# Where VectorE's small work stands between a kernel's matmuls: seven moves in one instruction order

## The chip, the cores and the metric

One NeuronCore of a Trainium2 chip runs the whole kernel. The metric is the device time of one execution in microseconds (us). The kernel before takes 943.9 us (median of three runs, 943.89 to 946.26).

A core has engines that run at the same time, each through its own list of instructions: TensorE multiplies matrices (PE in the profile, PEld for its weight loads), VectorE (DVE) does elementwise work, reductions and 32x32 block transposes, ScalarE (ACT) exponentials and copies, GpSimd (POOL) here mostly indirect DMAs, and SyncE (SP) issues DMAs. They wait for one another by semaphores. SBUF is the working memory; TensorE writes its results to PSUM, from where VectorE or ScalarE reads them.

## The reference

Attention in which a query sees only the keys of its own cluster, followed by a two-layer network with a PReLU. There are 4 batches, 8 heads, 768 tokens, head size 64 and 16 clusters for each head.

```python
q_assign = argmax(normalised(q) @ normalised(centroids).T)      # and k_assign, for each head
mask = q_assign[:, :, :, None] == k_assign[:, :, None, :]
scores = where(mask, q @ k.T / 8, -1e9)
attn = softmax(scores)                                          # over the keys
x = heads_side_by_side(attn @ v)                                # 3072 x 512
h = x @ w_in                                                    # 512 x 2048
out = (maximum(h, 0) + alpha * minimum(h, 0)) @ w_out           # 2048 x 512
```

## The kernel before, in words

**Pairs and steps.** Two heads of one batch make a pair; pair n is heads 2(n%4) and 2(n%4)+1 of batch n//4, so there are 16. Pairs 0 to 9 are worked on as they lie, once for each half of the queries. Pairs 10 to 15 are first sorted by cluster ("whole" or "near" pairs), so that each chunk of 128 keys meets only a window of the queries around it. The order of the work is written out by hand as 78 steps u, three to a pair and half (or to a whole pair). Steps 0 to 23 are batch 0; 24 to 47 batch 1; 48 to 53 pairs 10 and 11; 54 to 65 pairs 8 and 9; 66 to 77 pairs 12 to 15. TOGETHER is 24.

**Slots.** A step is divided into slots. In each slot `tick()` first runs what was put off with `later(k, piece)` (k ticks ahead), then come VectorE's pieces of attention, then `feed(pieces)`, which issues pieces of the network of earlier rows, then `prepare(u, slot)`, which issues what `prep_at` holds for that place. In the first step of a pair from step 24 on there are three ticks around the scores and only two such slots, and there `prepare` comes right after the tick, for places 2 and 3 (FIRST is 2): what is put at place 2 has no network piece of its step ahead of it, and what is put at place 3 comes behind those that the first slot feeds. How many pieces a slot feeds is worked out so that a block's pieces are spread evenly over its slots (L1557 to L1559). A hidden piece is one of 16 column blocks of w_in (8 matmul instructions, L1063) with a copy by ScalarE (L1069) and a slope by VectorE (L1055); a final piece is 8 instructions of L1081.

**Attention of a pair.** The scores (L781) go to PSUM, ScalarE takes exponentials (L799, L802), VectorE masks (L822) and adds up (L832, L860, L864), turns the sums (L870) and reduces them (L878). At the head of the next pair's first step TensorE folds the sums (L891), VectorE inverts them (L904) and spreads them (L911), TensorE weighs the values (L936, or L969 for whole pairs) and VectorE multiplies both (L1039, L975).

**Clusters.** `prep_blocks` (L364) transposes the queries and keys of a pair, `prep_sims` (L381) multiplies them by the centroids into the PSUM bank "mps", and one tick later VectorE takes the argmax (L402 to L408). The pool of mps has one buffer; `misc()` hands it out, and its next user waits until its last reader is done. Whole pairs are ordered ahead of time: step ORDERS[n-10] loads them, the next transposes them (`order_features`, L565), the one after multiplies (`order_sims`, L573) and takes the argmax piece by piece in the following slots; eight and nine ticks on come a transpose and a running count (L587), then `order_begins` (L599), `order_ranks` (L607 to L609), `order_rows` (L616 to L620) and `order_clusters` (L637 to L643). GpSimd scatters their rows by these numbers (L673), a few in each slot, paced by tiny copies of ScalarE and GpSimd (L649, L650).

**Back to rows.** The result of a whole pair is turned on TensorE through mps (`to_rows`, L999, six ticks after the pair is normalised), copied by ScalarE one tick later (L1002), scattered back (L1008), fetched, and turned by VectorE (L1027).

**Checks.** The kernel's short cuts hold only if the inverses lie in a range and sorted clusters do not spread too far. `check_inverses` (L340, two reductions) keeps the smallest and largest of a batch, and the end combines all into a flag (L1582 to L1635) that decides whether a general version must run.

**The last batch.** Its network runs as a scheme with seven products instead of eight, after the attention. In `last_pieces`, `hidden(x)` for x = 0 to 7 has the products p1, p5, p2, p6, p3, p7 and, put off to the next x's p2, p4 (L1241). Their results are copied by ScalarE (L1173) or added by VectorE (L1176), then sloped (L1181), and p7 also issues sums for later products (L1220, L1229, L1126). After x = 7, `room_for_y` issues p4 at once. The final products follow (L1297).

## Time and profile before

| what | us |
|---|---|
| median of three runs | 943.9 |
| the profiled execution, its own time | 944.23 |
| its span, from the first to the last instruction | 942.5 |
| TensorE busy | 924.1 |
| VectorE busy | 663.5 |
| GpSimd busy | 351.2 |
| ScalarE busy | 265.9 |

The granted TensorE clock is 0.999 of full speed over the span. Busy times are averages over stages that differ. In the table by stage VectorE is busy for 22.47 of the 24 us from 448 to 472, 9.82 of the 10 from 472 to 482, 20.93 of the 24 from 508 to 532 and 55.76 of the 74 from 789 to 863; TensorE for 24.00, 7.91, 22.42 and 73.05 of them. Step 51 begins near 470 us, step 54 near 508, step 57 near 532, and the last batch's network at 789.

In the timeline and in groups of instructions a line names engine, source line, operation, what is written and read, and the number of instructions; in brackets stand the engine's idle time before it and what ended it. A matmul in fp32 is two instructions. The ends of matmuls are modelled, so their starts say more.

### The profile page before, as it was taken

Reading aid. Unit: us, or ns where it says so; the run is one execution under the profiler, and the core shown is the slowest. Engines: PE = TensorE matmul, PEld = TensorE weight load, DVE = VectorE, ACT = ScalarE, POOL = GpSimd, SP = SyncE. Lnnn points to the kernel's source line nnn. Section 1 sums busy time; section 2 is a strip of 40 time slices with the busy share of each in tenths; the row PEclk is TensorE's granted clock in tenths of the full one; section 3 lists DMA queues with packets and bytes.
Section 4 is the critical chain, followed back from the end, with each engine's and each line's share of the span. In section 5 each row is a group of like instructions: output and inputs, shape, how many; then the busy total and the mean of one; then the engine's idle time right before and its main releaser. Section 6 shows DMA issues by size and latency. Waiting matters only on the chain.

```text
span 942.5 us, 11891 instructions
## 1 busy us (share of the span) xinstructions
PE 924.1 (98%) x3995; PEld 496.5 (53%) x3995; DVE 663.5 (70%) x1247; ACT 265.9 (28%) x658; POOL 351.2 (37%) x529
## 2 busy tenths in 40 slices
PE   8999999999999999999999999999999999999997
PEld 5534444445455454454544545545455555556886
DVE  5797788799679589698995955456888535698100
ACT  5764444323123032331322322223133121221000
POOL 2333222200016576467534686364256670000000
PEclk9999999999999999999999999999999999999999
DMA  8333658039001645165920134333441112000000
GB/s 297 125 127 96 146 130 149 18 59 198 1 6 53 159 87 133 47 120 131 155 52 12 43 80 101 63 67 62 93 75 34 32 37 53 1 0 1 23 23 26
DMA packets 209668, 73.38 MB, mean 78 GB/s; under 512 B 194288, under 2 KB 198080, under 8 KB 209600
## 3 DMA queue, kind: packets, MB, share of 16 engines
q1 hardware_dynamic: 201840, 60.35, 29.2%
q0 software_dynamic: 6912, 11.81, 4.1%
q8 instruction: 33, 0.54, 0.2%
q10 hardware_dynamic: 848, 0.39, 0.2%
q14 instruction: 35, 0.29, 0.1%
HBM read 49.89 MB, written 22.28 MB: 77 GB/s over the span
## 4 chain that ended last, share of the span: by engine, by line
PE 87%; DVE 6%; SPq 2%; DMA 2%; issue 1%; POOL 1%; ACT 1%; ACTq 0%; DVEq 0%; POOLq 0%
PE fps L1081 26%; PE fps L1063 25%; PE vps L936 7%; PE sps L781 7%; PE sps L1297 4%; PE sps L1241 4%; PE fps L781 2%; PE vps L1297 2%; PE vps L1241 2%; PE fps L1297 1%; PE fps L1241 1%; PE sps L790 1%; PE vps L969 1%; PE mps L969 1%; PE mps L381 1%
## 5 line engine op out<-in xcount | busy, mean ns | idle before, releaser
L1063 PE MATMUL fps<-xT,w_in_sb 128*128 128x384 f32 x768 | 257.7, 490 | 0.0
L1081 PE MATMUL fps<-w_out_sb,gT 128*128 128x512 f32 x576 | 254.4, 595 | 1.1 <-DVE gT L1055 1.1
L1063 PEld LDWEIGHTS fps<-xT,w_in_sb 128*128 128x128 f32 x768 | 142.8, 190 | 102.6 <-issue 3.8
L1081 PEld LDWEIGHTS fps<-w_out_sb,gT 128*128 128x128 f32 x576 | 107.5, 190 | 133.4 <-issue 123.0
L673 POOL DMA_INDIRECT scratch<-stage,off x144 | 155.4, 1079 | 49.7 <-issue 25.1
L650 POOL COPY paced<-pace 1x1 f32<-1x1 f32 x196 | 55.5, 283 | 202.3 <-ACT pace L649 201.5
L1069 ACT COPY gT<-fps 128x384 f32<-128x384 f32 x96 | 46.0, 479 | 215.6 <-PE fps L1063 215.6
L1055 DVE SCALAR_TENSOR_TENSOR gT<-gT,alpha 128x384 f32<-128x384 f32 x96 | 61.3, 648 | 50.4 <-ACT gT L1069 50.3
L781 PE MATMUL sps<-qkT 64*128 64x384 f32 (+1 forms) x480 | 88.6, 487 | 0.0
L1008 POOL DMA_INDIRECT back<-rows,found x72 | 74.9, 1040 | 18.2 <-issue 16.1
L802 ACT ACTIVATE E<-sps 128x768 f32<-128x768 f32 (+1 forms) x78 | 57.9, 790 | 59.4 <-PE sps L790 38.8
L781 PEld LDWEIGHTS sps<-qkT 64*128 64x128 f32 x480 | 42.7, 186 | 40.5 <-issue 15.0
L822 DVE SCALAR_TENSOR_TENSOR more<-aq,key,more 128x384 f32<-128x384 bf16 (+2 forms) x120 | 63.0, 584 | 1.2 <-ACT more L799 1.1
L936 PE MATMUL vps<-E,vt 128*64 128x384 f32 x316 | 58.6, 495 | 1.4 <-DVE xT L1039 1.4
L904 DVE RECIPROCAL inverses<-mps 64x12 f32<-64x12 f32 (+1 forms) x44 | 10.9, 248 | 58.5 <-PE mps L891 58.1
L822 DVE SCALAR_TENSOR_TENSOR E<-aq,key,E 128x384 f32<-128x384 bf16 (+2 forms) x96 | 50.2, 577 | 1.9 <-ACT E L799 1.8
L271 POOL TENSOR_TENSOR w_in_sb<-w_in_sb,power 128x512 f32<-128x512 f32 x16 | 25.1, 1573 | 67.8 <-DVE w_in_sb L268 67.8
L832 DVE TENSOR_TENSOR acc<-acc,E 128x768 f32<-128x768 f32 x37 | 35.3, 953 | 14.7 <-ACT E L802 13.6
L271 POOL TENSOR_TENSOR w_out_sb<-w_out_sb,power 128x512 f32<-128x512 f32 x16 | 22.9, 1434 | 57.3 <-DVE w_out_sb L268 57.3
L802 ACT ACTIVATE more<-sps 128x768 f32<-128x768 f32 (+1 forms) x42 | 31.1, 775 | 33.1 <-PE sps L781 32.0
L1087 ACT COPY y<-fps 128x512 f32<-128x512 f32 x18 | 10.6, 586 | 99.1 <-PE fps L1081 99.1
L1089 DVE TENSOR_TENSOR y<-y,fps 128x512 f32<-128x512 f32 x24 | 16.4, 683 | 29.1 <-PE fps L1081 29.1
(283 smaller groups left out, 1167.2 us busy)
## 6 DMA issues: line engine op xcount, KB each, us to landing
raw<-in_moe_w_in_dram SPq DMA_DIRECT2D x16, 512.0 KB
raw<-in_moe_w_out_dram SPq DMA_DIRECT2D x16, 512.0 KB
out_dram<-y SPq DMA_DIRECT2D x21, 256.0 KB
qk<-in_q_dram SPq DMA_DIRECT2D x48, 96.0 KB
qk<-in_k_dram SPq DMA_DIRECT2D x48, 96.0 KB
qk<-scratch SPq DMA_DIRECT2D x48, 96.0 KB
w_in_kept<-w_in_sb SPq DMA_DIRECT2D x8, 512.0 KB
vt<-in_v_dram SPq DMA_DIRECT2D x10, 384.0 KB
```

The costliest lines, as they stand in the source:

```text
L650: nc.gpsimd.tensor_copy(out=sorts["paced"], in_=token)
L673: nc.gpsimd.indirect_dma_start(out=scratch[n][1][h * NX + xx], out_offset=bass.IndirectOffsetOnAxis(ap=ranks[n][:, xx, h:h + 1], axis=0), ...
L781: nc.tensor.matmul(out=bank(ps, h, m), lhsT=qkT[r:r + D, S + c * P:S + (c + 1) * P], rhs=qkT[r:r + D, tokens], start=True, stop=not early_ ...
L802: nc.scalar.activation(out=E[:, :, 0:m], in_=ps[:, :, 0:m], func=AF.Exp, scale=SCALE)
L822: nc.vector.scalar_tensor_tensor(out=e, in0=of, scalar=keys[n][:, NJ + c, h:h + 1], in1=e, op0=ALU.is_equal, op1=ALU.mult)
L936: nc.tensor.matmul(out=po[r:r + D, 0:HS], lhsT=vts[n][:, h, c, :], rhs=e[:, h, :], start=(c == 0), stop=(c == NJ - 1))
L1008: nc.gpsimd.indirect_dma_start(out=to[i], out_offset=bass.IndirectOffsetOnAxis(ap=place[:, h, j:j + 1], axis=0), in_=rows[j // HJ][:, j % ...
L1055: nc.vector.scalar_tensor_tensor(out=gs[f], in0=gs[f], scalar=alpha[:, f:f + 1], in1=gs[f], op0=ALU.mult, op1=ALU.max)
L1063: nc.tensor.matmul(out=ps[:, 0:HS], lhsT=w_in_sb[:, c, f * P:(f + 1) * P], rhs=xTs[b, half][:, c, :], start=(c == 0), stop=(c == NCH - 1))
L1081: nc.tensor.matmul(out=ps[:, 0:DM], lhsT=gs[f][:, i * P:(i + 1) * P], rhs=w_out_sb[:, f, :], start=on and f == f0, stop=off and f == f0 + ...
L1241: nc.tensor.matmul(out=bank[to], lhsT=w_in_form(m, x, cc), rhs=rhs[:, cc, :], start=start and cc == 0, stop=cc == KH - 1, skip_group_check ...
L1297: nc.tensor.matmul(out=bank[to], lhsT=g_form(m, x, t), rhs=w_out_form(n, x), start=start and x == 0, stop=x == NQ - 1, skip_group_check=no ...
```

## The change

Nothing is computed otherwise; instructions of VectorE, with what belongs to them, stand at other places.

- The range check of a batch is issued three ticks after the last inverse of that batch is asked for, at steps 24, 48 and 66. Before, it was issued when the first inverse of the next batch was asked for, just ahead of it, at steps 27, 51 and 69. The last batch's check stays at the end.
- The transposes of pair 6 (`prep_blocks` at step 23) go one slot later.
- The similarities of pairs 8 and 9 (`prep_sims` at steps 48 and 51) go from place 2 to place 3.
- The ordering of pair 15 begins at step 53 instead of 50: its eight loads, two transposes, similarities, argmax, count, ranks, rows and clusters all come three steps later.
- In the last batch's network the slopes of f1 are issued after p7's sum instead of p3's.
- The final check's small operations are spread between network pieces: eight pieces, not one, are fed before the `feed(8)` ahead of the flag.

```diff
-    kept_of = [0]
+    kept_of, inverted = [0], [0] * B
 
     def inverse(n, half):
 
-        if pairs[n][0] > kept_of[0]:
-            check_inverses()
+        b = pairs[n][0]
+        inverted[b] += 1
+        if inverted[b] == 2 * NCH and b < B - 1:
+            later(3, check_inverses)
         return inverses[:, (2 * n + half) % (2 * NCH), :]
...
             def p3():
                 plus(g_of(f1, 1), product("e", "S4", x_of(1, 1), False))
-                slopes(f1)
 
             def p7():
                 plus(g_of(f2, 1), product("a", "S3", x_of(1, 0), False))
+                slopes(f1)
                 late.append(p4)
...
-    ORDERS = [26, 29, 35, 38, 41, 50]
+    ORDERS = [26, 29, 35, 38, 41, 53]
...
                 for w in range(2):
-                    at(u - 7, FIRST + w, lambda n=n, w=w: prep_blocks(n, w))
+                    at(u - 7, FIRST + w + (u - 7 == TOGETHER - 1),
+                       lambda n=n, w=w: prep_blocks(n, w))
             at(u - (3 if n < NCH else 5 if u - 6 < TOGETHER else 6), FIRST,
-               lambda n=n: prep_sims(n))
+               lambda n=n: prep_sims(n)) if u - 6 < 2 * TOGETHER else at(
+                   u - 6, FIRST + 1, lambda n=n: prep_sims(n))
...
     sum_x(slice(0, 4))
+    feed(2)
     good = const.tile([P, 2], FP32, name="good")
     check_inverses()
+    feed(1)
     nc.vector.tensor_reduce(out=good[:, 0:1], in_=highest, axis=AX.X, op=ALU.max)
...
                             scalar2=good[:, 0:1], op0=ALU.is_ge, op1=ALU.mult)
+    feed(1)
     nc.vector.tensor_reduce(out=good[:, 0:1], in_=alpha, axis=AX.X, op=ALU.max)
...
-    feed(1)
+    feed(2)
     nc.vector.tensor_copy(out=spans.rearrange("p i n -> p (i n)"), in_=ps[0:m, 0:4 * NN])
...
+    feed(2)
     tiles = const.tile([m, 2, NN], I32, name="tiles")
```

## The prediction

> **What bounds the kernel now.** I read the page's first part, then TensorE's waits, then the timeline and the chain around the longest of them. From the page:

> ```profile
> PE 924.1 (98%) x3995; PEld 496.5 (53%) x3995; DVE 663.5 (70%) x1247; ACT 265.9 (28%) x658; POOL 351.2 (37%) x529
> ```

> TensorE sets the end. A piece of its work that waits for nobody cannot be shortened by another order, so the change can save no more than TensorE's waits for others. All of over 0.8 us (columns: waiter, released by, total us, times, longest):

> ```profile
> PE fps L354 <- ACT qkT L358: 1.6, 2, 1.5
> PE mps L599 <- DVE simT L587: 1.6, 1, 1.6
> PE vps L936 <- DVE xT L1039: 1.4, 1, 1.4
> PE vps L201 <- POOL ident masks.py:199: 1.4, 1, 1.4
> PE mps L381 <- DVE qk L975: 1.2, 1, 1.2
> PE fps L1081 <- DVE gT L1055: 1.1, 2, 0.9
> PE sps L1241 <- DVE gT L1176: 0.9, 1, 0.9
> PE mps L969 <- DVE inverses L904: 0.9, 1, 0.9
> ```

> Five of them (1.6, 1.2, 0.9, 0.9, 0.9, together 5.5 us) lie behind VectorE where the diff touches its order; the other three are in the first 70 us, where it changes nothing. The two around 475 us, in the timeline (start, length, engine, line, idle before and its releaser):

> ```profile
> 473.12 0.58 DVE L1055 SCALAR_TENSOR_TENSOR gT<-gT,alpha 128x384 f32<-128x384 f32 x1
> 473.62 0.25 DVE L340 TENSOR_REDUCE lowest<-inverses 128x1 f32<-128x96 int32 x1
> 473.78 0.24 DVE L340 TENSOR_REDUCE highest<-inverses 128x1 f32<-128x96 int32 x1
> 474.13 0.62 DVE L904 RECIPROCAL inverses<-mps 64x24 f32<-64x24 f32 x2
> 474.90 1.79 PE L969 MATMUL mps<-E,vt 128*64 128x384 f32 x16 [0.93 <-DVE inverses L904]
> 479.01 0.55 DVE L975 TENSOR_TENSOR qk<-mps,rd 128x384 f32<-128x384 f32 x1
> 479.61 0.85 PE L381 MATMUL mps<-qkT,cT 128*32 128x384 f32 x8 [1.16 <-DVE qk L975]
> ```

> The one PSUM bank "mps" ties both: the weighing of L969 and the similarities of L381 may not write it before VectorE has read it. The chain of work has the same picture at 194.59 and 861.68, VectorE just ahead of TensorE:

> ```profile
> 193.00 0.94 DVE qkT L364
> 193.94 0.51 DVE gT L1055
> 194.45 0.14 issue
> 194.59 1.96 PE fps L1081 x4
> ```

> [...] L904 starts only after both L340. [...] L381 starts 0.05 us after L975 ends. [...] the trace has 557 (L975) and 949 to 954 (L832). [...] I count starts: a 384-column instruction follows its predecessor by 0.322 us when nothing waits.

> **The change part by part**, in the profiled execution's time (944.23 us; span 942.5, 1.7 around it). Steps and slots are those told above.

> (a) Pair 6's two transposes (L364, 0.94 us each) go one slot later in step 23. The first no longer stands ahead of the slopes L1055. VectorE's reduction L878 ends at 192.59, L477 takes it to 193.08, the first slope ends at 193.6, TensorE resumes 0.15 later as now: 193.76 for 194.59, **0.83**. Behind this VectorE carries the same work; it waited 0.52 us for TensorE at 210.27 and 0.96 at 225.83, so the lead is kept.

> (b) The check of batch 1 (two L340) leaves the front of L904 at step 51: L1055 ends at 473.70, L904 could start at 473.66 for 474.13, **0.47**; 0.44 of the wait stays, because VectorE has no idle stretch over 0.1 us from 455 on. Its new place is step 48, after the first masks, where VectorE idled 0.36 us before L402 at 454.34; the two overlapping reductions need 0.36. Without that cover it would cost what it gains. The checks of batches 0 and 2 stood and will stand where VectorE is ahead of TensorE (it waited 0.96 us behind the first of them): nothing; with that cover gone, 0.36 each.

> (c) Pair 9's similarities go to the second slot of step 51. The first slot feeds one hidden piece there: after slot k of block 48 to 60 there remain 2 + ceil(26(47-k)/48) pieces, 22 at k=11, 21 at 12, 21 at 13. So 2.58 us of L1063 come ahead of L381; their PSUM banks are free, ScalarE's L799 being done at 478.22. L381 would have started at 478.51 (0.42 after the last score, as at an unstalled change of line): 479.61-478.51, **1.10**. Pair 8 at step 48 feeds nothing between its two places: nothing. Its argmax then follows the mask of chunk 4, the same sum on VectorE. Next to want mps after L381 is L999 two slots on, at 484.1 by then; VectorE's L402, freed of the transposes of (d), has read it by 482.5.

> (d) Pair 15's ordering goes from steps 50-55 to 53-58. The scan L587 (0.95) leaves step 54, so L599's wait there goes: it would have started at 516.1 for 517.74, **1.64**. It returns at step 57, where slot k=36 feeds a hidden piece (9 to 8 left) ahead of it. VectorE there: removed from 54-56 are scan 0.95, ranks 0.9, rows 1.3, clusters 1.45, together 4.6; added are two L565 of 0.96 and L402 to L410 at 0.58+0.55+0.59+0.36+0.55+0.54, together 5.1. Followed slot by slot, the scan would end near 541.9, L599 be reached near 542.3: no wait, by 0.4 us. But a new wait comes at step 55, slot 2: its rows (L999) are turned through mps, no piece is fed (13 left at k=27 and 28), and the moved similarities L573 want mps next. ScalarE's copy L1002 frees it 0.57 us after L999's end by 521.42+0.49 against 521.33, behind the copy L1069; L573 would start at 521.96 for 521.17, **-0.79**. Bounds: 0.45 if L1002 were not behind L1069, 0.95 with another entry ahead of it. All of TensorE's later work is queued behind L573; VectorE, full there, uses the time. The eight loads move on SyncE past the staging loads of step 51; their issue (0.5 to 0.7 each) then lies in steps 51-53 where nothing is staged, about 30 us before their use. The scatters don't move: pair 14's are 27 of the 51 after 543 us, and pair 15's begin near 600.

> (e) slopes(f1) goes from p3 behind p7's sum. Only for the last x is p4 right behind p7: L1176 could start at 860.84 (0.59 after p7's last matmul start, as at 859.55) for 861.08, and TensorE gains 0.23. The slopes, which now fill a hole, come after it, so the rest of VectorE's list runs 0.85 later: the last T1 (L1229, 871.95) ends at 872.8, when TensorE wants it (869.98+14*0.216=873.0, less 0.23). Between 0 and 0.23: **0.15**. For the other x the sums come earlier and VectorE's least margin (1.4 us, p3's sum at x=3) stays positive with 0.8 off.

> (f) The final check's 23 small operations (0.14 to 0.28 each, 4.5 us with their gaps from 789.62 to 794.12) go between the sums of six products of TensorE. It takes 1.29 us for each product and never waited from 790 to 859; at most nine of them, some 1.5 us, now stand ahead of one sum (p7's, at 797), whose reader p4 comes 3.9 us after the product's end. So nothing; without that cover, up to 0.3. The four matmuls L1596 (0.4 us) and L1632 only change place on TensorE.

> Sum: 0.83+0.47+1.10+1.64-0.79+0.15 = 3.40, so 940.83 for that execution. It was 0.33 over the median; from the median, 943.9-3.4 = **940.5**.

> **Rivals.**
> 1. More: L573's wait is short and all else holds: 4.2, 939.7. For it: L1002 takes only 0.49. Against it: L1069 is just ahead of it.
> 2. Given back: TensorE runs early into stretches where VectorE is full (22.5 of 24 us in 448-472, 20.9 of 24 in 508-532). If VectorE is 1 us later at step 57 than I count, L599 waits 0.6; if the check of batch 1 finds no hole, (b) is gone; with (e) at 0 the gain is 3.4-0.6-0.47-0.15, about 2.2: 941.7, no measurable change.
> 3. Slower: L1002 stuck behind ScalarE's pacing copies. ScalarE waited 5.1 us for GpSimd in three such copies at 551 to 555. If that happened just ahead of L1002 at step 55, L573 would wait 5.1 us more: 945.6. It decides when GpSimd is eight copies behind at 519 us; the timeline has it three behind, so it is unlikely.
> 4. A late load of pair 15 would hold VectorE's whole queue at L565; it would have to land 30 us late. Left out.

> **How the numbers follow.** A run tells about 0.3% from no change, 2.8 us: the line is 941.1. My case (940.0 to 941.3) 0.56, the first rival 0.15, the second 0.23, the third 0.06. The first is faster, nine tenths of mine too (a tenth of it lies past the line), and a little of the second; the second otherwise the same, and half of the third. Faster 0.68, same 0.28, slower 0.04. The range runs from 939.4 (all bounds good) to 942.6, which leaves out the third and the worst of the second.

> **What would show it.** Right: TensorE's waits of L599 and L381 gone, L969's about 0.4, L1081's 0.4 in all, L1241's 0.7, and a new one, L573 on ScalarE's L1002, of 0.6 to 0.9. Wrong: L969's wait unchanged (no hole at step 48), a wait of L599 near 540 us, one of L1297 near 872 us, or no wait at L573.

## The result and the profile after

The changed kernel took 941.44 us (median of 7 runs, 940.28 to 941.87) against 944.05 us (7 runs, 943.86 to 946.27): a ratio of the means of 0.9963, 95% interval 0.9952 to 0.9974. The medians alone stand at 0.9972: two of the seven runs of the kernel before took 946.26 and 946.27, about 2 us more than its other five; the experiments on part d come back to this. Forecast were 940.5 us and a range of 939.4 to 942.6; the median also lies just above the 941.1 that the forecast took for the line between a gain that one can tell and none. The profiled execution took 941.45 us (span 939.7) against 944.23 (span 942.5), 2.78 less where the sum said 3.40.

In the changed file every line from about 335 on stands two lower: L383 is the old L381, L575 the old L573, L906 L904, L971 L969, L1083 L1081, L1243 L1241. From the page after:

```profile
PE 925.5 (98%) x3995; PEld 497.9 (53%) x3995; DVE 664.1 (71%) x1247; ACT 265.9 (28%) x658; POOL 348.2 (37%) x529
```

TensorE still sets the end, with the same instructions. Its waits, those the forecast spoke of (waiter, released by, total us, times, longest):

```profile
PE sps L1243 <- DVE gT L1178: 0.6, 1, 0.6
PE mps L575 <- ACT rows L1004: 0.6, 1, 0.6
...
PE fps L1083 <- DVE gT L1057: 0.3, 1, 0.3
PE mps L971 <- DVE inverses L906: 0.3, 1, 0.3
```

The ordering's L599 (1.6) and the similarities' L381 (1.2) no longer wait for VectorE, a new wait stands at L575 as foretold, and L971 waits 0.26 where 0.44 was foretold. The timeline around 475 us (start, length, engine, line, idle before and its releaser):

```profile
472.67 0.57 DVE L1057 SCALAR_TENSOR_TENSOR gT<-gT,alpha 128x384 f32<-128x384 f32 x1
473.16 0.61 DVE L906 RECIPROCAL inverses<-mps 64x24 f32<-64x24 f32 x2
...
473.92 1.79 PE L971 MATMUL mps<-E,vt 128*64 128x384 f32 x16 [0.26 <-DVE inverses L906]
...
477.40 1.56 PE L1065 MATMUL fps<-xT,w_in_sb 128*128 128x384 f32 x4
...
478.03 0.55 DVE L977 TENSOR_TENSOR qk<-mps,rd 128x384 f32<-128x384 f32 x1
```

The reciprocals follow the slopes without the check between them, and a hidden piece (L1065) runs on TensorE while VectorE's L977 reads the bank that L383 wants. The new wait, same view:

```profile
515.78 0.49 PE L1001 MATMUL mps<-ident,qk 128*128 128x128 f32 x3
...
515.98 0.48 ACT L1071 COPY gT<-fps 128x384 f32<-128x384 f32 x1 [1.58 <-PE fps L1065]
...
516.35 0.49 ACT L1004 COPY rows<-mps 128x384 f32<-128x384 f32 x1
...
516.89 1.06 PE L575 MATMUL mps<-qk,cT 128*32 128x384 f32 x8 [0.62 <-ACT rows L1004]
```

L1004 stands behind the copy L1071, which is the place of it that the forecast took. The chain of work at 194 us (start, length, what) shows TensorE following itself, where a transpose of VectorE stood in it before:

```profile
192.57 1.72 PE fps L1083 x4
194.29 0.00 issue
194.29 1.95 PE fps L1083 x4
```

To see where the time went I set each of TensorE's instructions in one trace beside the same one in the other and took the difference of their starts. Before minus after, so a growing number is a gain:

| place | us | difference | part of the forecast | forecast | measured |
|---|---|---|---|---|---|
| start | to 150 | -0.56 | none | 0 | -0.56 |
| L1083 | 194 | +0.30 | a | 0.83 | 0.86 |
| L971 | 474 | +0.97 | b | 0.47 | 0.67 |
| L383 | 483 | +2.01 | c | 1.10 | 1.04 |
| L575, L601 | 515-545 | +2.74 | d | 0.85 | 0.73 |
| p4, T1 of the end | 859, 873 | +3.04, then +2.89 | e | 0.15 | 0.30 - 0.15 |
| final check | 790-860 | no step | f | 0 | 0 |

The moves gave 3.45, all kept to the end; 0.56 of that was lost in the first 40 us, where the change edits nothing. In the rows for 483 us and on, instructions that themselves moved to another place are left out, and each difference is taken where the same work has been done in both. Of the 0.67 at 474 us only part is b's own; the experiments take it apart.

### The profile page after: what moved, and what is told of

It reads as the page before. It is cut to its first block, busy times and chain, and to the rows that moved or that the text cites. A ratio compares the mean times of both kernels' runs of the same rounds, so it can differ in the third digit from the quotient of the medians.

```text
span 939.7 us, 11886 instructions
## 1 busy us (share of the span) xinstructions
PE 925.5 (98%) x3995; PEld 497.9 (53%) x3995; DVE 664.1 (71%) x1247; ACT 265.9 (28%) x658; POOL 348.2 (37%) x529
## 4 chain that ended last, share of the span: by engine, by line
PE 91%; DVE 7%; issue 1%; ACT 0%; POOL 0%; DVEq 0%; ACTq 0%; POOLq 0%
PE fps L1083 26%; PE fps L1065 25%; PE vps L938 8%; PE sps L783 7%; PE sps L1243 4%; PE sps L1299 4%; PE fps L783 3%; PE vps L1243 2%; PE vps L1299 2%; PE fps L1299 1%; PE fps L1243 1%; PE mps L971 1%; PE vps L971 1%; PE sps L792 1%; PE mps L893 1%
## 5 line engine op out<-in xcount | busy, mean ns | idle before, releaser
L1065 PE MATMUL fps<-xT,w_in_sb 128*128 128x384 f32 x768 | 258.3, 490 | 0.0
L1083 PE MATMUL fps<-w_out_sb,gT 128*128 128x512 f32 x576 | 253.9, 595 | 0.3 <-DVE gT L1057 0.3
L1065 PEld LDWEIGHTS fps<-xT,w_in_sb 128*128 128x128 f32 x768 | 142.6, 190 | 103.5 <-issue 3.8
L1083 PEld LDWEIGHTS fps<-w_out_sb,gT 128*128 128x128 f32 x576 | 107.7, 190 | 132.9 <-issue 122.5
L1071 ACT COPY gT<-fps 128x384 f32<-128x384 f32 x96 | 45.9, 478 | 214.9 <-PE fps L1065 214.9
L906 DVE RECIPROCAL inverses<-mps 64x12 f32<-64x12 f32 (+1 forms) x44 | 10.9, 247 | 62.0 <-PE mps L893 61.7
L271 POOL TENSOR_TENSOR w_in_sb<-w_in_sb,power 128x512 f32<-128x512 f32 x16 | 22.6, 1410 | 71.1 <-DVE w_in_sb L268 71.1
```

The costliest lines, as they stand in the source:

```text
L1065: nc.tensor.matmul(out=ps[:, 0:HS], lhsT=w_in_sb[:, c, f * P:(f + 1) * P], rhs=xTs[b, half][:, c, :], start=(c == 0), stop=(c == NCH - 1))
L1083: nc.tensor.matmul(out=ps[:, 0:DM], lhsT=gs[f][:, i * P:(i + 1) * P], rhs=w_out_sb[:, f, :], start=on and f == f0, stop=off and f == f0 + ...
```

## The experiments

Losses and gains below are changes of this difference of starts across a place, against the profile of the changed kernel. A single time says little here: undo_a, undo_b and undo_c lose 0.86, 0.31 and 1.19 us by their starts and all have the changed kernel's span of 939.7. Their first 40 us were shorter (by 0.64, 0.22 and 0.99), and so was the stretch behind the last matmul (by about 0.2).

**Part a undone.**

```
-                    at(u - 7, FIRST + w + (u - 7 == TOGETHER - 1),
+                    at(u - 7, FIRST + w,
```

> The changed kernel with pair 6's transposes back in their old slots of step 23, all else as changed. The parts-add-up theory: TensorE's wait for the slopes at about 194 us comes back (0.9 longer), and everything TensorE does after it is 0.83 to 0.90 us later than in the changed kernel, to the end. The rival (the lead of part a is given back further on, where VectorE is full): later by 0.8 at 200 us, but by less than 0.4 at the end.

The difference goes from -0.64 to +0.22 at 194 us and stays there to the end: 0.86 lost, nothing given back. Part a stands alone.

**Part b undone, part c undone, both undone.** The first edit puts back the checks of batches 0, 1 and 2 alike; the one that TensorE waits for at 474 us is that of batch 1.

```
-        if inverted[b] == 2 * NCH and b < B - 1:
-            later(3, check_inverses)
+        if pairs[n][0] > kept_of[0]:
+            check_inverses()
```
```
-               lambda n=n: prep_sims(n)) if u - 6 < 2 * TOGETHER else at(
-                   u - 6, FIRST + 1, lambda n=n: prep_sims(n))
+               lambda n=n: prep_sims(n))
```

> The changed kernel with the range check of batches 0 and 1 back in front of the next batch's first reciprocal. The parts-add-up theory (each part acts alone): TensorE's wait for the reciprocals at 474 us grows by 0.47 to 0.67, from 0.26 to 0.7 or 0.9. The rival: VectorE is one unbroken queue from 453 to 473 us, so a check taken out of it at 453.6 (0.32 from start to start) makes the queue arrive 0.32 earlier, and one put in at its end costs 0.5: the wait grows by only 0.2, to 0.4 to 0.5, and the gain of part b was really that of the 0.44 gap ahead of the pair's argmax, which is filled by the check and, through part c, by two masks.

> The changed kernel with the similarities of pairs 8 and 9 back in the first slot. Parts-add-up: the wait of pair 9's similarities for VectorE's product is back with 1.1 to 1.2, all later work is 1.1 us later, and the wait for the reciprocals at 474 us stays 0.3. The rival (parts b and c share one gap of VectorE at 454 us: without c two masks no longer come ahead of pair 8's argmax): the wait for the reciprocals grows as well, to 0.4 to 0.5, and 1.2 to 1.35 are lost in all.

> Both parts b and c undone. Both theories: as before the change in this place, the wait for the reciprocals 0.9 and that of pair 9's similarities 1.1 to 1.2, in all 1.75 to 1.85 us later after 485 us than the changed kernel. If the parts are independent, this is the sum of the losses of the two single runs; if they share the gap, the single runs' losses add to something else (0.2 and 1.3).

| undone | L971's wait | lost at 474 | lost at 483 | together |
|---|---|---|---|---|
| nothing (changed kernel) | 0.26 | | | |
| b | 0.57 | 0.31 | 0 | 0.31 |
| c | 0.42 | 0.16 | 1.03 | 1.19 |
| b and c | 0.93 | 0.68 | 1.04 | 1.72 |

The losses alone add to 1.50, together they are 1.72: b and c share something at 474 us. Neither expectation of undo_b was right (0.47 to 0.67, or 0.2), that of the rival nearer; undo_c came as its rival said, but for 0.01, and undo_bc 0.03 under what both said. VectorE's timeline says what is shared. Before the change:

```profile
452.96 1.02 DVE L822 SCALAR_TENSOR_TENSOR E<-aq,key,E 128x320 f32<-128x320 bf16 x2 [0.64 <-ACT E L799]
454.34 0.58 DVE L402 STREAM_TRANSPOSE simT<-mps 128x384 f32<-128x384 f32 x1 [0.36 <-PE mps L381]
```

After it:

```profile
452.67 1.01 DVE L824 SCALAR_TENSOR_TENSOR E<-aq,key,E 128x320 f32<-128x320 bf16 x2 [0.64 <-ACT E L801]
453.60 0.24 DVE L342 TENSOR_REDUCE lowest<-inverses 128x1 f32<-128x96 int32 x1
453.76 0.24 DVE L342 TENSOR_REDUCE highest<-inverses 128x1 f32<-128x96 int32 x1
453.92 1.14 DVE L824 SCALAR_TENSOR_TENSOR E<-aq,key,E 128x384 f32<-128x384 bf16 x2
454.98 0.57 DVE L404 STREAM_TRANSPOSE simT<-mps 128x384 f32<-128x384 f32 x1
```

With c undone:

```profile
451.68 1.02 DVE L824 SCALAR_TENSOR_TENSOR E<-aq,key,E 128x320 f32<-128x320 bf16 x2 [0.64 <-ACT E L801]
452.61 0.25 DVE L342 TENSOR_REDUCE lowest<-inverses 128x1 f32<-128x96 int32 x1
452.77 0.25 DVE L342 TENSOR_REDUCE highest<-inverses 128x1 f32<-128x96 int32 x1
453.05 0.58 DVE L404 STREAM_TRANSPOSE simT<-mps 128x384 f32<-128x384 f32 x1
```

Without c, pair 8's argmax (L402, now L404) comes right behind two masks and waits 0.36 us for TensorE. The check drops into this gap, L404 starts 0.03 us after it, and the gain of b is 0.52 (0.68 - 0.16). With c the argmax stands two masks later: work that was due after it now fills the gap, check or no check, and VectorE's queue, which has no idle stretch over 0.04 us from there to L906, arrives 0.16 us earlier than with the check alone. So c is worth 0.16 at 474 us too, or 0.37 (0.68 - 0.31) where b is not made.

**The check of batch 2 left out at its place.**

```
-        if inverted[b] == 2 * NCH and b < B - 1:
+        if inverted[b] == 2 * NCH and b < B - 2:
...
     check_inverses()
+    check_inverses()
```

> The changed kernel without the range check of batch 1 at its place in step 48; it is made at the end, on what the inverses hold then, so that the denominators of batch 1 go unchecked. If VectorE's queue from 453 to 473 us is unbroken, the wait for the reciprocals at 474 us goes from 0.26 to nothing and 0.2 to 0.3 us are gained from there on. If the check lies wholly in a gap of the queue (the recorded estimate), the wait stays 0.26.

There are four batches, so this edit takes away the check of batch 2, not that of batch 1 as I had meant. One more check at the end reads what the inverses hold then, so that batch 2's go unchecked. The reductions at 453.9 us are still in the trace. So the run says nothing on batch 1. It does show that batch 2's check is hidden: the difference is +0.34 before and +0.36 after its place. What batch 1's check still costs is shown by the last experiment (0.20 us).

**Part d undone, twice.**

```
-    ORDERS = [26, 29, 35, 38, 41, 53]
+    ORDERS = [26, 29, 35, 38, 41, 50]
```

> The changed kernel with pair 15's ordering begun at step 50 again instead of 53. My theory: the wait of the similarities behind ScalarE's copy near 517 us (0.62 us) goes, the wait of 1.6 us behind the ordering's scan near 515 to 520 us returns, and TensorE is later by 0.7 to 0.85 us from 545 us to the end. The rival (the old ordering's work, VectorE's transposes, now falls on the similarities of pair 9 or on the later ones, or the new one frees more than the two waits show): a new wait for VectorE between 480 and 515 us of over 0.2 us, and a loss of 1 us or more.

> The kernel of undo_d again, since TensorE ran at half its pace from 517.5 to 521.1 us there, which hid the size of part d. My theory: with no such stretch, 0.7 to 0.95 us later than the changed kernel from 545 us on, counted from its lead at 480 us: a wait of 1.74 for the scan's result, and none of 0.79 for ScalarE's copy. The rival (the half pace belongs to this order of work): the same stretch again.

The wait of 1.58 us for the scan returns in both and L575's goes. But both lose 2.42 us between 484 and 560 us, far over what I had expected, and both have a stretch where the instructions of a hidden piece follow each other at 0.64 us in place of 0.32. So undo_d2 showed the same stretch again, as its rival had said. From its timeline:

```profile
515.07 0.58 PE L601 MATMUL mps<-simT,row 128*128 128x1 f32 x4 [1.58 <-DVE simT L589]
515.51 4.52 PE L1065 MATMUL fps<-xT,w_in_sb 128*128 128x384 f32 x8
```

Its windows (from:to, length, then the busy time of PE, PEld, DVE, ACT and POOL with their instructions, PEclk the granted clock, DMA share, GB/s):

```profile
513.06:516.47 3.41, 1.83 (x11) 1.12 (x8) 3.41 (x8) 1.68 (x6) 1.34 (x3) 1.00 0.00 0
516.47:519.88 3.41, 3.41 (x7) 1.62 (x6) 3.38 (x9) 0.00 (x0) 2.86 (x4) 0.50 0.06 19
```

```profile
516.49:519.90 3.41, 2.16 (x10) 1.53 (x11) 3.41 (x10) 0.90 (x4) 1.96 (x4) 1.00 0.03 10
519.90:523.31 3.41, 3.41 (x14) 2.15 (x13) 3.34 (x7) 0.86 (x2) 2.25 (x3) 1.00 0.06 19
```

63% busy, and nothing followed; in its second profile a border fell into the same wait too (65%), and again nothing followed. So the order of work alone does not bring the stretch about, against undo_d2's rival. Half of 3.41 is 1.71; taken from 2.42 that leaves, as an estimate, 0.71 for the order of work, near the 0.73 by which the changed kernel gained there on the kernel before. So the old place of pair 15's ordering cost 2.42 us where a stretch at half clock followed, and 0.73 where none did. The kernel before may show it in its times: of its 11 runs beside these experiments, three had a mean granted clock of 0.997, as undo_d and undo_d2 have, and took 946.27, 946.53 and 946.53 us; eight had 0.998 or 0.999 and took 944.00 to 945.55. Those three runs have no trace, so that a stretch at half clock lies here in them is argued, not shown.

**Part e undone; part f undone.**

```
                 plus(g_of(f1, 1), product("e", "S4", x_of(1, 1), False))
+                slopes(f1)
...
                 plus(g_of(f2, 1), product("a", "S3", x_of(1, 0), False))
-                slopes(f1)
```

For f, the products between the final check's small operations go back to where they were: the added feed(2), feed(1), feed(1) and feed(2) leave, and the feed ahead of the copy of spans is 1 again.

> The changed kernel with the first slopes back in p3, ahead of p7's sum. My theory: the wait for p7's sum grows from 0.6 to 0.9 near 859 us (0.25 to 0.3 later), and half of it comes back at the last T1 near 873 us, so 0.10 to 0.20 us later at the end. The rival (VectorE's list is ahead at the end and nothing is given back): 0.25 to 0.3 later at the end as well.

> The changed kernel with the final check's small operations together again, as before the change. My theory: TensorE's starts differ by less than 0.05 us from 800 us to the end, since VectorE is ahead of TensorE there in both. The rival (the check is not hidden): 0.1 to 0.3 us later from 800 us on.

Part e: 0.30 lost at 859 us (2.04 to 2.34), 0.15 back at 873 (2.19), so 0.15 at the end, as the forecast had it. Part f: 3.55 before the check and 3.56 to the end, nothing. Both runs, and undo_d, had another loss at 478 us, where TensorE's hidden piece waits for ScalarE's L801: 0.8 us in undo_d, 2.0 in undo_e and 2.2 in undo_f. In undo_e's timelines ScalarE and VectorE both resume at 478.3, though TensorE had started the matmuls that they wait for by 475.5, at full clock by the record. A like loss of 0.6 came at 697 us in these three and in the kernel before, which ran with them on one chip, and in no other profile. What held them up stays open. It is not the edits: those of undo_e and undo_f touch nothing before 780 us, and undo_d2, the same kernel as undo_d on another chip, has neither loss.

**Both kernels once more.**

> The kernel before, unchanged, once more. My theory of the start: the first 30 us differ from one execution to the next by up to about 1.2 us, for the same instructions, by when TensorE's clock is granted in full (first seen: 4.5 us after the start before the change, 7.3 us after it), and from 40 us on the two executions of this kernel run alike to within 0.05 us. The rival (the start of 0.6 us more belongs to the change): the start is that of the first profile of this kernel.

> The changed kernel once more, as the partner of the other runs of this call. My theory: beyond the first 30 us its starts agree with the first profile of it to a constant within 0.1 us, and its time against the kernel before is 0.9963 again, within 0.0012. The rival (the gain belongs to the chip): a ratio outside this.

Kernel before: 0.4 us ahead of its first profile from 40 to 696 us, constant within 0.05, then the 0.6 of 697 us. Kernel after: constant at +0.19 to +0.22 from 40 us on, and 940.82 us against 944.45, a ratio of the means of 0.9956 (0.9942 to 0.9969), as was expected. The start varies by itself. In before_again the first 10 us were like those of its first profile; the variation is shown by the other runs, whose code is the same up to 190 us. In the kernel before's first profile L201's matmuls start 0.213 us apart ahead of the grant of full clock and 0.111 behind it. In the profiles an execution whose grant comes 1 us earlier is about 0.5 us ahead at 10 us, up to about 1 us in all: it came at 7.34 us in the first profile of the changed kernel, at 6.90 in undo_b (0.22 ahead), 6.05 in undo_a (0.64), 5.01 in undo_c (0.99) and 4.49 in the first profile of the kernel before (0.98). After that, waits near 29 to 31 us took back 0.3 to 1.1 us in some runs of either kernel. Among the profiles of kernels that are the same up to 190 us, the same instructions near 100 us start at times over 1.6 us apart. Nothing of this belongs to the change; of its 3.45 us it hid 0.56 in the two profiled executions.

**Three moves more.**

```
-            at(t + 2, 2, lambda n=n: order_sims(n))
+            at(t + 2, 2 + (n == NP - 1), lambda n=n: order_sims(n))
```
```
-            later(3, check_inverses)
+            later(1 if b else 3, check_inverses)
```
```
         def room_for_y():
-            late.popleft()()
...
-            for x in (NQ - 2, NQ - 1):
-                g_sums(x)
-            for x in (NQ - 2, NQ - 1):
-                w_out_sums(x)
+            g_sums(NQ - 2)
+            w_out_sums(NQ - 2)
...
             while late:
                 late.popleft()()
+            if t == 0:
+                g_sums(NQ - 1)
+                w_out_sums(NQ - 1)
```

> The changed kernel with three more moves: pair 15's similarities one slot later in step 55, behind a hidden piece; the last p4 behind the final layer's first product; the range check of batch 1 two slots earlier in step 48, where VectorE waits 0.6 us for ScalarE. My theory, from the stalls left in the changed kernel: 0.79 at 517 us, 0.65 at 859 us and 0.15 at 870 us, and 0.26 at 474 us, together 1.85 us ahead of the changed kernel from 880 us on, so about 939.6. The rival (VectorE's queue is the bound in these stretches, and what TensorE gains at one place it waits at the next): a wait for the ordering's scan near 540 us or for the last sums near 872 us, and under 1 us in all.

It took 940.23 us (5 runs) against 940.82 for the changed kernel on the same chip; both stand to the kernel before at ratios whose intervals overlap (0.9950, 0.9936 to 0.9963). By the starts it is 0.50 ahead, where 1.85 was expected; the rival was right that it would be under 1, but the wait came at another place than it had named. The similarities behind a hidden piece gain 0.90 at 517 us and L575's wait is gone. The check in VectorE's other gap, the 0.64 at 452 us, gains 0.20 and leaves L971 a wait of 0.05. The third move loses 0.60:

```profile
PE fps L1299 <- DVE gT L1183: 1.4, 1, 1.4
```

The final layer's second product reads what the late p4 makes, through ScalarE's copy and VectorE's slopes, which now come behind the sums of the last x but one. I had looked at p5 as the next reader; it is the product ahead of it. The first two moves without the third would be 1.10 ahead of the changed kernel by these starts; that was not run.

## Why the prediction was right, point by point

**(a), (e), (f)** came as worked out: 0.86 for 0.83; 0.30 for 0.23 at p4, with half returned, which leaves 0.15 for 0.15; nothing for nothing.

**(b)** was right for what it does alone: 0.52 for 0.47, L971's wait at 0.42 for 0.44, the check whole in the 0.36 us hole. What failed is a step of **(c)**, "Pair 8 at step 48 feeds nothing between its two places: nothing. Its argmax then follows the mask of chunk 4, the same sum on VectorE." The sum of the work is the same, but not the idle time in it: with its argmax behind two masks, VectorE no longer waits at this hole. So 0.16 us at 474 were left out of the forecast. The rest of (c), at step 51, gave 1.04 for 1.10.

**(d)** had the right mechanism with both terms: L599's wait goes, L573's comes behind L1002, which is itself behind L1069. Measured were 0.73 for 0.85. By the starts, L599's term came whole: the difference goes from 2.99 to 5.08 across it, of which 0.45 is its own time and comes back at its new place; 1.64 is left. Across L575 it goes from 5.08 to 3.19, of which 0.98 is L575's own time. So the new wait cost 0.91 for 0.79, which is all of the 0.12; the run "best", which removes this wait, gains 0.90. (The 0.62 in the timeline counts from the modelled end of L1001.) L601 met no wait at step 57, but by far more than the 0.4 us counted: the scan L589 ended at 537.56 and L601 started at 540.03, 2.5 us later, so VectorE was some 2 us further ahead there than counted. What the forecast did not have at all is that L599's wait can be followed by 3.41 us at half clock, as in undo_d and undo_d2, which lost 2.42 us there, so that its removal is worth more in some executions than in the profiled one.

**The sum**: 3.45 for 3.40. That it came so close is in part luck: 0.20 too little at 474 us stood against 0.06 and 0.12 too much in (c) and (d). The changed kernel's time of 941.44 is nevertheless 0.9 over the forecast, and the term in question is the first one, "from the median, 943.9-3.4": a shift of the start by 1 us and more from one execution to the next was in neither the sum nor the reasons of the range. The changed kernel's seven runs spread over 1.6 us by themselves, and against the kernel before, the medians differ by 2.6 us in the result and by 3.6 when both ran once more.

**The rivals.** More (939.7): L573's wait came, and L1069 was ahead of L1002, as was said against it. Given back (941.7): its number is nearer to the median than mine, its mechanism (a wait at step 57, no hole at step 48) did not come. Slower: no pacing copy stood ahead of L1002; ScalarE's idle 1.58 us ahead of L1071 was for TensorE. A late load did not come: VectorE's two transposes of pair 15 (L567, at 513.67 and 515.59) had no idle ahead of them.

## What to carry to other kernels

That the sum of work in an in-order queue stays the same does not make a move in it free (two masks ahead of an argmax were worth 0.16 us here): ask which idle stretch of that queue it fills or opens, and count two edits that touch one stretch together. Judge sub-microsecond moves by the starts of the same instructions in two traces, not by the end-to-end time, which here moved by 1 us and more through the start alone. Before a product is moved behind another, list every reader of what it makes, the next one first.

## What the runs showed of the hardware

A wait of 1.58 us that fell wholly into one stretch of 3.41 us, counted from the first grant of full clock (TensorE 54% busy in it), was followed by half clock for the next 3.41 us, in two profiles of two (undo_d, undo_d2). The same wait spread over two stretches was not, in two of two (the kernel before's; the emptier stretch 63% and 65% busy). The price was 1.71 us, an estimate from half the 3.41. In these four profiles it went by where the stretches lie, and that differs from one execution to the next: the grant came between 4.47 and 7.34 us in the profiles for which it is given here.

The busy share of a stretch does not settle it alone. Stretches of 55% to 63% at other waits were followed by full clock in every trace, but so were two just before the end, of 51% (undo_d2, at 932.9 us) and of 54% (after_again, at 931.3 us). What in a stretch decides stays open.
